# Moving one weight's loads to a second DMA queue in the head of a fused attention and MLP kernel

## The chip, the cores and the metric

The kernel runs on one core of a Trainium2 chip. A core has TensorE (PE in the profile; its weight loads are listed apart as PEld), VectorE (DVE), ScalarE (ACT), GpSimd (POOL) and SyncE (SP). SyncE and ScalarE can both start transfers; here, before the change, SyncE starts all of them. The metric is the device time of one execution in microseconds; smaller is better.

## The reference

Inputs are bfloat16: x of 2048 rows and 512 columns, four 512x512 weights, three weights of a gated MLP with inner width 1792, a vector beta of 32 and a vector gate_w of 512.

```python
x = A_x
g = sigmoid((x * gate_w).sum(-1, keepdims=True))
q, k, v = x @ wq, x @ wk, x @ wv          # 32 heads of 16, 4 segments of 512 rows
for s in range(4):                        # within a segment: causal softmax attention
    a_dot = softmax(q_s k_s^T / 4 + mask) v_s
    a_mem = phi(q_s) M / (phi(q_s) z + 1e-6)      # memory of the segments before
    o_s = sigmoid(beta) * a_mem + (1 - sigmoid(beta)) * a_dot
    M, z = M + phi(k_s)^T v_s, z + sum(phi(k_s))
a = concat(o) @ wo
b = (gelu(x @ w_gate) * (x @ w_up)) @ w_down
out = g * a + (1 - g) * b
```

## The kernel before

Everything works on segments of 512 rows, with x held transposed in the tiles `x0` to `x2`: 128 partitions, 4 chunks `fc` of the 512 columns, 512 rows. Each product with x (`u_k`, `u_q`, `u_v`, `u_gate`, `u_up`) is a group of four matmuls over `fc` into one PSUM bank, and then a copy out of it. A planner in Python, with its own estimates of costs and due times, writes down the order of the instructions of each engine once the head is over; in the head the order is that of the calls. Each engine runs its list in order, and semaphores tie the lists together.

The head is this. `load_inputs` (L136) starts the transfers, all on SyncE: segment 0 of x in two halves of 256 rows, into a borrowed tile `G`; the columns 0 to 255 and 256 to 511 of wk; wq; gate_w; wv; beta; and w_gate in two parts. `cols` (L133) is the helper for weights: a weight's rows are spread over the partitions, so that one contiguous piece is a run of columns of one row: 512 bytes for a half of wk, 1024 bytes for wq, wv and the first part of w_gate, while x comes in pieces of 2048 bytes, beta in pieces of 64 bytes. `warm_up` (L163) gives TensorE matmuls on constants. `transpose_x0` (L177) turns x's two halves with eight TensorE transposes each (tile `x0T`), and per half one VectorE copy (L189) and one ScalarE copy (L191) bring them to SBUF. ScalarE's first instruction is the table load that its first copy needs. Then come three groups with wk (`kT`, L376; groups 0 and 1 read half 0 of wk, group 2 reads half 1), four groups with wq (`qT`, L290), the transposition of gate_w (L195), four groups with wv (`vT`, L414), a narrow group (`zT`, L430), `setup_beta` (L215), which begins with an exponential on ScalarE (L217), and 14 groups with w_gate (`gT`, L473). The later loads, x of segments 1 and 2, w_up, w_down and wo, are started by `load_rest` behind a small VectorE memset (L152).

Eight semaphores are used in turn by the transfers, so the ninth transfer in the program's order waits until the first has landed, the tenth for the second, and so on: the first part of w_gate waits for x's first half, x of segment 1 for the third transfer.

Of the kernel before, what the change touches and what calls it, by code (L numbers as in the profile page):

```python
# [13 lines left out]
P = 128  # L14
D = 512
H = 32
# [16 lines left out]
F32 = dt.float32  # L33
# [20 lines left out]
def kernel(  # L54
# [15 lines left out]
    nc = tc.nc  # L70
# [4 lines left out]
    x2 = A_x[0]  # L75
# [8 lines left out]
    def const(shape, dtype, name):  # L84
        return cpool.tile(shape, dtype, name=name, tag=name)
# [3 lines left out]
    wk = const([P, FC, D], BF, "wk")  # L89
# [8 lines left out]
    beta = const([P, H], BF, "beta")  # L98
# [22 lines left out]
    hm = const([P, 8], F32, "hm")  # L121
# [11 lines left out]
    def cols(dst, src):  # L133
        nc.sync.dma_start(dst[:, :, :], src.rearrange("(fc p) n -> p fc n", p=P))

    def load_inputs():  # L136
        half = L // 2
        for i in range(2):
            nc.sync.dma_start(x0[:, 2 * i:2 * i + 2, :],
                              x2[half * i:half * (i + 1), :].rearrange("(p k) d -> p k d", p=P))  # L140
        for i in range(2):
            n = slice(D // 2 * i, D // 2 * (i + 1))
            cols(wk[:, :, n], A_wk[:, n])
        cols(wq, A_wq)
        nc.sync.dma_start(gw4, gate_w.rearrange("(fc p) -> fc p", p=P))
        cols(wv[:, :, 0:D], A_wv)
        nc.sync.dma_start(beta[:, :], A_beta.rearrange("(o n) -> o n", o=1).to_broadcast((P, H)))
        for n in (slice(0, 4 * P), slice(4 * P, DFF)):
            cols(wga[:, :, n], B_w_gate[:, n])

# [10 lines left out]
    gw4 = G[1][0:FC, KT, 0:P]  # L161
# [535 lines left out]

    ctx.enter_context(tc.manual_schedule())
    load_inputs()
    make_identity(nc, ident[:, :])  # L700
    warm_up()
# [289 lines left out]
    for pieces in visits:  # L991
# [17 lines left out]
        if lumps and lumps[0][0] == clock[0]:  # L1009
            i = lumps.pop(0)[1]  # L1010
# [5 lines left out]
        n = len(visits) - clock[0]  # L1016
# [150 lines left out]
    for reg in flag:  # L1167
        i = 0 if reg.engine == mybir.EngineType.Pool else 1
# [32 lines left out]
```

## Time and profile before

| What | us |
|---|---|
| Median of 3 runs | 269.65 (269.63 to 270.01) |
| Profiled execution, its own time | 270.29 |
| Its span in the profile | 268.6 |
| TensorE busy | 263.5 |
| First transpose of x, first kT matmul, first qT matmul start at | 3.77, 6.05, 9.11 |

The span is the time from the first to the last recorded instruction; the execution's own time holds some more around it. Times in the views are counted from the span's start. A busy TensorE is not TensorE at its peak, since matmuls are pipelined. A row of the timeline gives start, duration, engine, line, operation, output and input, and in brackets the idle time before it and what ended that. SPq rows are the instructions on SyncE that start a transfer; ACTq would be the same on ScalarE.

### The profile page before, as it was taken

The page shows a single profiled execution, that of the slowest core. Times are in us where ns is not written, and L with a number is a line of the kernel's source. Part 1 is how long each engine was busy: PE and PEld are TensorE (multiplying, and loading weights), DVE is VectorE, ACT ScalarE, POOL GpSimd, SP SyncE. Part 2 cuts the span into 40 slices and gives each one's busy share as a digit, 9 for nine tenths or more (in the row PEclk, how much of TensorE's full clock was granted, in tenths as well). Part 3 has the DMA queues.
Part 4 walks back from the last instruction along what each step waited for, and adds up shares of the span by engine and source line. Part 5 has one row for each costly group of instructions (what it writes and reads, how often), then busy time and mean ns, then how long its engine had stood idle before and what let it go on. Part 6 is the DMA issues. An engine that isn't in the chain of part 4 may idle for free.

```text
span 268.6 us, 6586 instructions
## 1 busy us (share of the span) xinstructions
PE 263.5 (98%) x2717; PEld 118.8 (44%) x2717; DVE 203.9 (76%) x392; ACT 209.1 (78%) x163; POOL 156.8 (58%) x298
## 2 busy tenths in 40 slices
PE   7999999999999999999999999999999999999994
PEld 4454444444454444544444444444454544444442
DVE  2899575958778787697985979686889479698374
ACT  4226889999997998889999988889888987657510
POOL 4000158897914979986920998596785069655500
PEclk9999999999999999999999999999999999999999
DMA  7999901200070000300042001100000300002102
GB/s 217 322 202 326 340 13 39 42 4 0 9 156 2 0 21 23 78 4 20 2 61 76 10 21 42 42 20 22 20 23 21 67 2 20 2 20 42 40 22 83
DMA packets 30409, 16.59 MB, mean 62 GB/s; under 512 B 20008, under 2 KB 29096, under 8 KB 30376
## 3 DMA queue, kind: packets, MB, share of 16 engines
q1 hardware_dynamic: 30376, 16.14, 23.1%
q8 instruction: 22, 0.36, 0.6%
q14 instruction: 11, 0.09, 0.1%
HBM read 8.14 MB, written 2.10 MB: 38 GB/s over the span
## 4 chain that ended last, share of the span: by engine, by line
PE 88%; POOL 5%; issue 4%; DVE 1%; ACT 1%; ACTq 0%; DVEq 0%; POOLq 0%
PE gT L473 19%; PE uT L494 17%; PE dT L510 14%; PE lg L649 8%; PE od L674 6%; PE qT L290 5%; PE kT L376 5%; PE aT L532 5%; PE vT L414 4%; POOL pT L658 3%; POOL KTm L386 2%; PE MT L559 1%; PE warm L166 1%; PE mn L628 1%; ACT pT L654 1%
## 5 line engine op out<-in xcount | busy, mean ns | idle before, releaser
L658 POOL TENSOR_SCALAR_AFFINE_SELECT pT<-pT 64x256 bf16<-64x256 bf16 x256 | 113.9, 445 | 94.8 <-ACT pT L654 81.9
L654 ACT ACTIVATE pT<-lg 128x2048 bf16<-128x2048 f32 x72 | 135.1, 1876 | 24.9 <-PE lg L649 21.6
L494 PE MATMUL uT<-x,wup 128*128 128x512 bf16 x224 | 60.4, 380 | 0.0
L473 PE MATMUL gT<-x,wga 128*128 128x512 bf16 x224 | 57.0, 380 | 0.0
L510 PE MATMUL dT<-wdn,G 128*128 128x512 bf16 x224 | 52.9, 380 | 0.0
L500 DVE TENSOR_TENSOR G<-uT,G 128x512 bf16<-128x512 f32 x56 | 38.1, 683 | 6.4 <-PE uT L494 6.2
L386 POOL TENSOR_SCALAR KTm<-ktb,eo 128x512 bf16<-128x512 bf16 x26 | 40.6, 1572 | 1.3
L681 DVE STREAM_TRANSPOSE oq<-od 128x512 f32<-128x512 f32 x32 | 21.0, 695 | 19.3 <-PE od L674 19.3
L510 PEld LDWEIGHTS <-G 128*128 128x128 bf16 x224 | 20.8, 98 | 25.0 <-issue 2.1
L473 PEld LDWEIGHTS <-wga 128*128 128x128 bf16 x224 | 20.4, 98 | 23.9 <-issue 2.2
L494 PEld LDWEIGHTS <-wup 128*128 128x128 bf16 x224 | 19.8, 97 | 24.0 <-issue 5.4
L649 PE MATMUL lg<-QT,KTm 32*128 32x192 bf16 (+7 forms) x512 | 28.6, 287 | 0.0
L313 DVE CAST G<-gT 128x512 bf16<-128x512 f32 x24 | 16.5, 687 | 9.8 <-PE gT L473 9.6
L649 PEld LDWEIGHTS <-KTm 32*128 32x128 bf16 x512 | 8.3, 92 | 28.4 <-issue 28.0
L674 PE MATMUL od<-pT,V 64*32 64x128 bf16 (+7 forms) x512 | 19.4, 284 | 0.2 <-POOL pT L658 0.2
L674 PE MATMUL od<-pT,Vs 64*32 64x128 bf16 (+7 forms) x512 | 19.4, 284 | 0.0
L488 ACT ACTIVATE G<-G 128x3584 bf16<-128x3584 bf16 x6 | 18.8, 3182 | 0.0
L687 DVE SCALAR_TENSOR_TENSOR o<-oq,ogs,rden 128x256 bf16<-128x256 f32 x32 | 17.0, 532 | 1.1
L376 PE MATMUL kT<-x,wk 128*128 128x512 bf16 x64 | 17.2, 388 | 0.4 <-DVE x L189 0.4
L290 PE MATMUL qT<-x,wq 128*128 128x512 bf16 x64 | 16.6, 379 | 0.0
L532 PE MATMUL aT<-wo,oT 128*128 128x512 bf16 (+1 forms) x68 | 16.5, 367 | 0.0
L538 DVE SCALAR_TENSOR_TENSOR tB<-aT,gct,tB 128x512 bf16<-128x512 f32 (+1 forms) x17 | 12.0, 714 | 6.0 <-PE aT L532 5.7
(96 smaller groups left out, 277.2 us busy)
## 6 DMA issues: line engine op xcount, KB each, us to landing
wup<-in_B_w_up_dram SPq DMA_DIRECT2D x1, 1792.0 KB, 8.3
wdn<-in_B_w_down_dram SPq DMA_DIRECT2D x1, 1792.0 KB
out_dram<-tB SPq DMA_DIRECT2D x13, 128.0 KB, 1.7
wga<-in_B_w_gate_dram SPq DMA_DIRECT2D x1, 1280.0 KB, 10.6
Vs<-V SPq DMA_DIRECT2D x8, 144.0 KB, 2.6
G<-in_A_x_dram SPq DMA_DIRECT2D x2, 256.0 KB, 3.0
wk<-in_A_wk_dram SPq DMA_DIRECT2D x2, 256.0 KB, 4.3
wq<-in_A_wq_dram SPq DMA_DIRECT2D x1, 512.0 KB, 5.9
```

The lines of the kernel that those rows point to most:

```text
L290: nc.tensor.matmul(T[:, :], lhsT=wq[:, fc, c * P:(c + 1) * P], rhs=xS[s % NX][:, fc, :], start=(fc == 0), stop=(fc == FC - 1))
L376: nc.tensor.matmul(T[:, :], lhsT=wk[:, fc, c * P:(c + 1) * P], rhs=xS[s % NX][:, fc, :], start=(fc == 0), stop=(fc == FC - 1))
L386: eng.tensor_scalar(out=KTm[:, (NC8 * s + c) % NK, :, p, :], in0=ktb[:, c, :].rearrange("q (b k) -> q b k", b=NB), scalar1=eo[:, p:p + 1], ...
L473: nc.tensor.matmul(T[:, :], lhsT=wga[:, fc, hs * P:(hs + 1) * P], rhs=xS[s % NX][:, fc, :], start=(fc == 0), stop=(fc == FC - 1))
L494: nc.tensor.matmul(T[:, :], lhsT=wup[:, fc, hs * P:(hs + 1) * P], rhs=xS[s % NX][:, fc, :], start=(fc == 0), stop=(fc == FC - 1))
L500: nc.vector.tensor_tensor(out=g, in0=T[:, :], in1=g, op=ALU.mult)
L510: nc.tensor.matmul(T[:, :], lhsT=G[s % NG][:, hs, qt * P:(qt + 1) * P], rhs=wdn[:, hs, :], start=(hs == 0), stop=(hs == HS - 1))
L532: nc.tensor.matmul(T[:, 0:w], lhsT=oT[:, fc, qt * P:(qt + 1) * P], rhs=wo[:, fc, d0:d0 + w], start=(fc == 0), stop=(fc == FC - 1))
L649: nc.tensor.matmul(lg[:, j, off:off + n], lhsT=KTm[rows, i % NK, b].rearrange("r p k -> r (p k)"), rhs=QT[rows, i % NC8, 64 * b:L], start= ...
L654: nc.scalar.activation(pT[:, :, :], lg[:, :, :], AF.Exp, scale=DH ** -0.5)
L658: nc.gpsimd.affine_select(out=v, in_=v, pattern=[[0, 4], [1, 64]], compare_op=ALU.is_ge, fill=0.0, base=0, channel_multiplier=-1)
L674: nc.tensor.matmul(od[p][32 * j:32 * j + 32, 64 * b:L], lhsT=w[:, 18 * h:18 * h + 32], rhs=t[rows, j, off:off + n], start=(b == 0), stop=( ...
```

## The change

In `load_inputs`, the two halves of wk are started by ScalarE, in ScalarE's own DMA queue, behind a copy of a zero into one column of the tile `hm`. SyncE starts x, gate_w and beta, then wq, wv and the two parts of w_gate. The other spelling of x's rearrangement describes the same pieces. All other instructions of all engines stay, in the same order.

```diff
         for i in range(2):
             nc.sync.dma_start(x0[:, 2 * i:2 * i + 2, :],
-                              x2[half * i:half * (i + 1), :].rearrange("(p k) d -> p k d", p=P))
+                              x2[half * i:half * (i + 1), :].rearrange("(p k) d -> p k d", k=2))
+        nc.scalar.copy(hm[:, 0:1], nc.const_aps.tensor(0.0, [P, 1], F32))
         for i in range(2):
             n = slice(D // 2 * i, D // 2 * (i + 1))
-            cols(wk[:, :, n], A_wk[:, n])
+            nc.scalar.dma_start(wk[:, :, n], A_wk[:, n].rearrange("(fc p) n -> p fc n", p=P))
+        nc.sync.dma_start(gw4, gate_w.rearrange("(fc p) -> fc p", p=P))
+        nc.sync.dma_start(beta[:, :], A_beta.rearrange("(o n) -> o n", o=1).to_broadcast((P, H)))
         cols(wq, A_wq)
-        nc.sync.dma_start(gw4, gate_w.rearrange("(fc p) -> fc p", p=P))
         cols(wv[:, :, 0:D], A_wv)
-        nc.sync.dma_start(beta[:, :], A_beta.rearrange("(o n) -> o n", o=1).to_broadcast((P, H)))
         for n in (slice(0, 4 * P), slice(4 * P, DFF)):
             cols(wga[:, :, n], B_w_gate[:, n])
```

## The prediction, on record before the run

> **What bounds the kernel now.** I read the page's first and third parts, then the chain of work that ended last, then the timeline of the first 17 us, then the transfers. Two lines of the page:
>
> ```profile
> PE 263.5 (98%) x2717; PEld 118.8 (44%) x2717; DVE 203.9 (76%) x392; ACT 209.1 (78%) x163; POOL 156.8 (58%) x298
> ...
> q1 hardware_dynamic: 30376, 16.14, 23.1%
> ```
>
> TensorE (PE) is busy 98% of the span. Once it has the first matmuls it hardly stops, so a microsecond that it loses in the head comes out at the end almost whole, and what the other engines or the queues gain there is worth nothing unless PE starts earlier. The second line shows one hardware queue for all transfers of the program: this trace has no stretch in which two queues share the DMA engines. The chain from its start to 13 us (start, length, what):
>
> ```profile
> 0.97 2.31 PE warm L166 x5
> 3.28 0.56 PE warm L172 x15
> 3.84 1.41 PE x0T L183 x12
> 5.25 0.02 issue
> 5.27 0.74 DVE x L189
> 6.01 0.04 issue
> 6.05 3.22 PE kT L376 x12
> 9.27 3.45 PE qT L290 x16
> ```
>
> Warm-up, 16 transposes of x (x0T), VectorE's second copy of x, 12 matmuls with wk (kT), 16 with wq (qT). There is no DMA in it. The timeline shows who issues which transfer and when, and what ScalarE (ACT) does:
>
> ```profile
> 0.79 0.87 SPq L139 DMA_DIRECT2D G<-in_A_x_dram  x2
> 0.85 1.28 ACT L191 ACT_TABLE_LOAD   x1 [0.85 <-PEq L1185]
> ...
> 1.71 0.97 SPq L134 DMA_DIRECT2D wk<-in_A_wk_dram  x2
> ...
> 2.73 0.51 SPq L134 DMA_DIRECT2D wq<-in_A_wq_dram  x1
> ...
> 4.84 1.58 ACT L191 COPY x<-x0T 128x512 bf16<-128x512 bf16 x2 [2.71 <-PE x0T L183]
> ...
> 10.90 0.23 ACT L217 ACTIVATE eb<-beta 128x32 f32<-128x32 bf16 x1 [4.48 <-DMA beta<-in_A_beta_dram]
> ```
>
> The view of one tile gives the times from issue to landing. For wk and for wq:
>
> ```profile
> DMA to landing us min/median/max: 3.5/4.3/5.1
> DMA to landing us min/median/max: 5.9/5.9/5.9
> ```
>
> The reader is to put a deadline beside each landing. x's halves are issued at 0.79 and 1.2 and take 2.8 and 3.1 us: landed at 3.6 and 4.3. The first transpose starts at 3.77, on the heels of the warm-up; the second half is wanted eight transposes later, at 4.60. Slack 0.2 and 0.3 us. wk half 0 is issued at 1.71, landed at 5.2, wanted for the matmul at 6.05: slack 0.85. Half 1 (columns 256 on, the third kT group) is issued at 2.2, landed at 7.3, wanted at 8.25: slack 0.95. wq lands at 8.63 and is wanted at 9.11: slack 0.5. So PE has just enough data at every step, and nothing in the head waits that could be removed.
>
> **The change, part by part.** What it removes: SyncE's queue (SP) no longer issues wk, 0.97 us. What it moves ahead of wq there are gate_w (0.45) and beta (0.50), together 0.95, so wq is issued where it was, at about 2.7. wv comes at about 3.3 instead of 3.78 and wga follows half a microsecond earlier. All of these have slack (wv is wanted at 12.76, wga at 16.28), so on PE's path this saves 0. x's own transfers are issued at the same instants, so x0T cannot start earlier; even with x there at once, the warm-up ends at 3.84. Gain of this part: 0 to 0.07 us; I take 0.
>
> Beta earlier: ACT's 4.48 us of idle time before L217 shrinks. What follows is a table load that then waits 4.91 us for PE, and VectorE uses the result at 17.01. Worth 0. If beta were late again, the cover is these 4.91 us.
>
> What it adds on ACT: a 128x1 copy, priced by the smallest ACT rows (L447, 128x4, 0.20 us; L217 0.23), and two DMA issues, priced by SP's (0.43 and 0.51), 1.2 us in all. Behind them stand the x copies of L191, which now start at 4.84 after 2.71 us of idle time: 1.2 fits, cost 0. The copy needs the table load, which is already the first thing ACT does, so the load moves nowhere. The later SP transfers that reuse wk's semaphore (x of segment 1 at 13.87) wait for a memset of VectorE at 13.77; wk has landed by then in every case below.
>
> What is left is when wk's transfers begin, and with whom they share the DMA engines. That is the whole price, and two numbers in it are not in this trace.
>
> First, the issue time. The new DMA instructions wait for no semaphore. The earliest is 0.85, when ACT starts; the latest is after the table load and the copy, 2.13 + 0.23 = 2.36. SP issued them at 1.71. Data begins about 1.0 us after an issue (x: issued 0.79, the first bytes in the slice of 1.8 to 2.0 us), so wk moves from 1.85 or from 3.36. I take the early end: nothing in the program ties the transfer to the copy's end.
>
> Second, the sharing. In the rows of half a microsecond the DMA engines move 45, 115, 340, 397, 316, 342, 278, 320 GB/s from 1.5 to 5.5 us, and on average 309 from 4 to 8 us: full, and in one order, x (524 KB), wk (524), wq (524). Added up, x is through at 3.74 and lands at 4.33, 0.6 later; wk half 0 is through at 4.53 and lands 0.7 later; half 1 at 5.41, and lands 1.9 later. With two queues wk no longer stands between x and wq but beside them. The ends: it loses nothing to the others and takes nothing from x, cost 0; or it takes half of the bytes from the first moment.
>
> - Early issue, half of the bytes: x's second half is through only when 1049 KB have moved, at 5.41, and lands at 6.0 instead of being ready for 4.60: PE 1.4 us later. wk itself then is in time.
> - Early issue, a fifth of the bytes beside x (x in 2 KB rows, wk in 512-byte rows, one row each in turn): x through after 655 KB, at 4.14, landed at 4.75, 0.15 late. Then wk stands beside wq's 1 KB rows and gets a third, 103 GB/s: half 0 at 5.4, landed 6.1, hidden; half 1 (262 KB, 2.5 us) at 7.95, landed 0.7 to 1.9 later, 8.65 to 9.85 instead of 8.25. PE 0.4 to 1.6 us later.
> - Late issue, half of the bytes: x 0.15 late, half 1 landed by 7.4 to 8.6: PE 0.15 to 0.35 later.
> - Late issue, a row each in turn: half 0 landed at 6.8, half 1 at 9.3 to 10.5: PE 0.75 to 2.25 later.
>
> For the early issue both shares end between 0.4 and 1.6, one through x and one through wk half 1. The 1.4 is too dear by half a microsecond, if PE's slow stretch (rival c) ends at 7.1 whenever kT starts: the 1.0 us from 6.05 holds only 0.5 us of work at full pace. So I take 0.9. wq gets past wk half 1 and is in time; wv and wga, issued earlier, add to what stands beside wk. Beta's 64-byte rows now run right behind x: in the stretch before it landed the rows fall to 176 to 223 GB/s (8.5 to 10 us), some 0.6 us of transfer lost, if beta is what did it. That would delay wq from 8.63 to 9.2, covered when kT is 0.9 late and costing 0.1 where it isn't.
>
> The sum for the profiled execution: span 268.6 + 0.9 = 269.5; its own time was 270.29, 1.69 more than its span, so 271.2. The median of the three runs, 269.65, is 0.64 below the profiled one: 269.65 + 0.9 = 270.55 us.
>
> [...]
>
> **The rivals.** (a) All of it is hidden, the other side: wk, issued early, gets through in the pauses of the first 2.5 us (45 and 115 GB/s, against 340 later), and both halves land before 6.05 and 8.25 without pushing x past 4.60. For it: slack of 0.85 and 0.95 us, which SP's issue time of 1.71 alone cannot fill. Against: from 2.5 us on the engines are full, and wk and wv, wga now compete. It decides at half 1 landing by 8.25. Price 0 to 0.3, time 269.65 to 269.95.
> (b) The copy does hold the issue back to 2.36, and wk, 0.65 us later than before and beside wq, is late for the first kT group: kT starts when half 0 lands, 6.8, and half 1 stops PE again. For it: wk half 1 already took 1.9 us from its last byte to its landing. Against: no wait in the program. Middle of 0.75 to 2.25: +1.5, 271.15.
> (c) Faster. PE's weight loads for kT start at 6.05, 6.43, 6.86, 7.17 and then every 0.22 us: the first three matmuls run slow. If all went at full pace, 0.47 us would be won, with the 0.07 of the transposes 0.54: just 0.2%. Nothing in the change works towards it, and a pause of PE more likely lengthens the slow stretch; 12 matmuls at 0.43 instead of 0.22 would cost 2.5.
>
> **How the numbers follow.** What a measurement of this kernel can tell from no change is about 0.2%, 0.54 us. Early issue with x or wk late, 0.4 to 1.6: chance 0.44, of which a tenth of the whole lies under 0.54. (b), 0.75 to 2.25: 0.21, all slower. (a): 0.25, all within 0.2%. (c) and what I can't name: 0.10. Slower 0.34 + 0.21 + 0.01 of the last, 0.56; within 0.10 + 0.25, 0.35; faster 0.09. The range: the low end, 269.4, leaves out most of (c); the high end, 271.9, is (b) at its 2.25, and leaves out the case that the slow stretch of PE grows too. The likeliest case's own range is 270.05 to 271.25.
>
> **What would show it.** The profile of after has a second hardware queue. The DMA issue on ACT begins before 1.3 (early) or after 2.1 (late). Right: x0T's second half or the third kT group starts late, with a wait for a DMA in front, and qT starts 0.9 later than 9.11. (a) is right if kT and qT start at 6.05 and 9.11. (b): PE's wait stands before the first kT matmul. I am wrong if wk lands earlier than at 5.2 and 7.3 while x keeps its 3.6 and 4.3, or if the difference arises behind 16 us, where I expect the same work in the same order.

## The result and the profile after

The changed kernel takes 271.55 us (median of 10 executions, 270.65 to 274.28), the kernel before 269.92 (10 executions, 269.63 to 270.46). The ratio is 1.0065, with an interval of 1.0044 to 1.0086: slower by 1.6 us. (The ratios take in all executions, so they differ from those of the medians where the executions form groups.) The forecast was 270.55, in a range of 269.4 to 271.9, with slower as the likeliest sign.

The profiled execution of the changed kernel is one of its faster ones: 270.83 us, span 269.1, against 270.29 and 268.6 before. The execution profiled before lies 0.37 over its own median. So the two profiles differ by only 0.5 us of the 1.6, and what the other executions add has to come from the experiments. Lines behind the change stand one lower than in the kernel before. Its page, parts 3 and 4:

```profile
q1 hardware_dynamic: 29320, 15.61, 22.6%
q10 hardware_dynamic: 1056, 0.52, 0.7%
...
PE 85%; POOL 5%; issue 4%; DMA 3%; ACT 1%; SPq 1%; DVE 0%; ACTq 0%; DVEq 0%; POOLq 0%
```

There is a second queue, q10, with wk's 0.52 MB, and a DMA in the chain of work that ended last, where there was none. The chain itself, from its start:

```profile
2.13 0.36 SPq L146
2.48 0.04 issue
2.53 7.00 DMA wq<-in_A_wq_dram
9.53 0.05 issue
9.57 3.63 PE qT L291 x16
```

PE's 16 wq matmuls wait for wq, issued at 2.53 and landed 7.00 us later. Before, wq was issued at 2.73 and took 5.9. The timeline of the head (start, duration, and in brackets the idle time before it):

```profile
0.92 1.00 ACTq L144 DMA_DIRECT2D wk<-in_A_wk_dram  x2
...
2.15 0.19 ACT L141 COPY hm<-const-float32-0.0 128x1 f32<-128x1 f32 x1
...
3.78 1.03 PE L184 MATMUL x0T<-ident,G 128*128 128x128 bf16 x8
...
5.26 0.88 PE L184 MATMUL x0T<-ident,G 128*128 128x128 bf16 x8 [0.45 <-DMA G<-in_A_x_dram]
...
6.68 2.75 PE L377 MATMUL kT<-x,wk 128*128 128x512 bf16 x12 [0.55 <-DVE x L190]
```

The same rows before:

```profile
3.77 1.89 PE L183 MATMUL x0T<-ident,G 128*128 128x128 bf16 x16
...
6.05 3.22 PE L376 MATMUL kT<-x,wk 128*128 128x512 bf16 x12 [0.39 <-DVE x L189]
...
9.11 3.62 PE L290 MATMUL qT<-x,wq 128*128 128x512 bf16 x16
```

wk's transfers are issued at 0.92, long before the copy that stands ahead of them runs at 2.15. The 16 transposes are torn in two: the second eight start at 5.26 instead of 4.60, behind a DMA wait on x. kT starts at 6.68 instead of 6.05. The landings, in the views of the tiles x is loaded into and wk:

```profile
DMA to landing us min/median/max: 2.9/3.5/4.0
DMA to landing us min/median/max: 3.5/4.0/4.5
```

x half 1, issued at 1.25, takes 4.0 us instead of 3.1. wk's halves, issued at 0.92 and about 1.4, land at 4.4 and 5.9: the first before x half 1 (5.25), both earlier than in the kernel before (5.2 and 7.3). Last, busy times and transfer rates by half a microsecond (the last number is GB/s):

```profile
4.50:5.00 0.50, 0.31 (x3) 0.04 (x1) 0.50 (x1) 0.15 (x1) 0.00 (x0) 1.00 1.08 326
5.00:5.50 0.50, 0.24 (x3) 0.25 (x4) 0.15 (x1) 0.50 (x1) 0.00 (x0) 1.00 1.74 138
5.50:6.00 0.50, 0.50 (x8) 0.50 (x6) 0.10 (x1) 0.08 (x1) 0.00 (x0) 1.00 0.59 77
6.00:6.50 0.50, 0.14 (x3) 0.02 (x1) 0.50 (x1) 0.33 (x1) 0.00 (x0) 1.00 0.24 81
6.50:7.00 0.50, 0.32 (x2) 0.19 (x2) 0.23 (x3) 0.40 (x1) 0.00 (x0) 1.00 0.60 209
```

Before, the three rows from 5 to 6.5 us were:

```profile
5.00:5.50 0.50, 0.50 (x7) 0.50 (x5) 0.38 (x2) 0.50 (x1) 0.00 (x0) 1.00 1.15 320
5.50:6.00 0.50, 0.16 (x2) 0.00 (x1) 0.50 (x3) 0.38 (x2) 0.00 (x0) 1.00 0.87 273
6.00:6.50 0.50, 0.45 (x2) 0.17 (x2) 0.10 (x2) 0.42 (x1) 0.00 (x0) 1.00 1.16 344
```

From 5 to 6.5 us, right when wq should be coming in, the engines move 77 to 138 GB/s instead of 273 to 344. The transfer that lies there is beta, landed 5.1 us after its issue at 2.13, at 7.2.

So there are two suspects: wk overtaking x half 1, and beta in front of wq. A third question comes from the spread: six executions of the changed kernel lie at 270.65 to 271.6, and four at 272.1 to 274.3. The slowest, 274.28, had a mean granted clock of 0.991, the other nine 0.998 to 1.0.

### The profile page after: what moved, and what is told of

Its sections match the earlier page's. It is cut to its first block, busy times and chain, and to the rows that moved or that the text cites. A ratio compares the mean times of both kernels' runs of the same rounds, so it can differ in the third digit from the quotient of the medians.

```text
span 269.1 us, 6587 instructions
## 1 busy us (share of the span) xinstructions
PE 263.2 (98%) x2717; PEld 118.4 (44%) x2717; DVE 204.2 (76%) x392; ACT 209.4 (78%) x164; POOL 157.3 (58%) x298
## 4 chain that ended last, share of the span: by engine, by line
PE 85%; POOL 5%; issue 4%; DMA 3%; ACT 1%; SPq 1%; DVE 0%; ACTq 0%; DVEq 0%; POOLq 0%
PE gT L474 19%; PE uT L495 17%; PE dT L511 14%; PE lg L650 8%; PE od L675 6%; PE qT L291 5%; PE aT L533 5%; PE vT L415 4%; PE kT L377 4%; POOL pT L659 3%; DMA wq<-in_A_wq_dram 3%; POOL KTm L387 2%; PE MT L560 1%; PE mn L629 1%; ACT pT L655 1%
## 5 line engine op out<-in xcount | busy, mean ns | idle before, releaser
L480 ACT ACTIVATE G<-gT 128x512 bf16<-128x512 f32 x14 | 8.4, 598 | 12.5 <-PE gT L474 12.5
## 6 DMA issues: line engine op xcount, KB each, us to landing
wga<-in_B_w_gate_dram SPq DMA_DIRECT2D x1, 1280.0 KB, 10.6
```

## The experiments

Each kernel was compared with the kernel before on its own chip; medians of before lay at 269.92 to 269.96. Where a spread is given, it is over all executions.

**e1: beta and gate_w back behind wq.** wk stays in ScalarE's queue.

```diff
-        nc.sync.dma_start(gw4, ...)
-        nc.sync.dma_start(beta[:, :], ...)
         cols(wq, A_wq)
+        nc.sync.dma_start(gw4, ...)
         cols(wv[:, :, 0:D], A_wv)
+        nc.sync.dma_start(beta[:, :], ...)
```

> wk stays in ScalarE's queue, gate_w and beta go back to their old places behind wq and wv. Theory (two causes: wk's early transfers push x half 1 back, and beta's 64-byte pieces in front of wq all but stop the transfers for 1.7 us): x half 1 still lands at about 5.2 and kT starts at about 6.7, but the rows of 5.0 to 6.75 us stay near 300 GB/s, wq lands before 9.2 and TensorE's wait in front of qT is gone; time 0.3 to 0.8 us over before, so about 1 us under the changed kernel. Rival (wk beside x and wq is the whole cause, beta's place is worth nothing): still 1.6 us over before.

Measured: 270.27 us, ratio 1.0037 (1.0018 to 1.0056), 0.32 over before. The profile (270.18 us):

```profile
5.20 0.62 PE L184 MATMUL x0T<-ident,G 128*128 128x128 bf16 x8 [0.39 <-DMA G<-in_A_x_dram]
...
6.41 2.75 PE L377 MATMUL kT<-x,wk 128*128 128x512 bf16 x12 [0.59 <-DVE x L190]
...
9.00 3.62 PE L291 MATMUL qT<-x,wq 128*128 128x512 bf16 x15
```

The torn x0T stays, the wait in front of qT is gone. That is what the theory of two causes expects; the rival, that beta's place is worth nothing, falls. wq is also issued 0.82 us earlier here (1.71 for 2.53); e6 below changes beta alone. But the executions make two groups: seven at 270.18 to 270.27, five at 271.77 to 272.07, and none between.

**e2: beta and gate_w ahead of wq in the kernel before, wk left on SyncE.**

```diff
+        nc.sync.dma_start(gw4, ...)
+        nc.sync.dma_start(beta[:, :], ...)
         cols(wq, A_wq)
-        nc.sync.dma_start(gw4, ...)
         cols(wv[:, :, 0:D], A_wv)
-        nc.sync.dma_start(beta[:, :], ...)
```

> The kernel before with gate_w and beta alone moved ahead of wq; wk stays in SyncE's queue. Theory (two causes): x half 1 lands at 4.3 and kT starts at 6.05 as before; the transfers all but stop for 1.0 to 1.7 us once wk is through, wq lands at 9.5 to 10.3 instead of 8.63, and qT starts 0.4 to 1.2 late; time 0.4 to 1.2 over before. Rival (wk's queue is the whole cause): within 0.2 us of before.

Measured: 271.01 us, ratio 1.0051 (1.0027 to 1.0076), 1.06 over before. Ten executions lie at 270.46 to 271.37, two at 272.62 and 274.49.

```profile
3.77 1.91 PE L183 MATMUL x0T<-ident,G 128*128 128x128 bf16 x16
...
6.07 3.15 PE L376 MATMUL kT<-x,wk 128*128 128x512 bf16 x12 [0.39 <-DVE x L189]
...
9.61 3.63 PE L290 MATMUL qT<-x,wq 128*128 128x512 bf16 x15 [0.39 <-DMA wq<-in_A_wq_dram]
```

x0T is whole and kT starts in time; qT waits for wq and starts 0.50 late. So this place makes the kernel slower without a second queue. But two things move together: wq is also issued 0.91 us later (3.64 for 2.73), and it lands 5.9 us after its issue in both kernels. The transfers do not all but stop, as was expected: they move 149 GB/s from 5.5 to 6 us and 197 to 245 up to 8.5, where the kernel before has 248 to 344. Which of the two costs the time, e2 does not tell.

**e3: e1 with the copy writing into wk, so that wk's transfers wait for it.**

```diff
-        nc.scalar.copy(hm[:, 0:1], nc.const_aps.tensor(0.0, [P, 1], F32))
+        nc.scalar.copy(wk[:, 0, 0:1], nc.const_aps.tensor(0.0, [P, 1], F32))
```

> As e1, but the small copy writes into wk, so that wk's transfers really wait for it. Theory (the plain copy holds nothing back, and an early wk pushes x half 1 back): the issue on ScalarE moves from 0.92 to about 2.4, x half 1 lands at 4.3 to 4.5 again and the second half of x0T has no wait; wk half 0 lands at 5.8 to 6.8, so kT starts between 6.05 and 6.8; time 0 to 0.7 over before, with the wait in front of kT instead of inside x0T. Rival (the wait inside x0T has another cause than wk): x half 1 still lands at 5.2 and the time is that of e1.

Measured: 274.64 us, ratio 1.0167 (1.0147 to 1.0187), 4.7 over before, far more than expected.

```profile
1.71 0.43 SPq L134 DMA_DIRECT2D wq<-in_A_wq_dram  x1
...
2.37 0.98 ACTq L144 DMA_DIRECT2D wk<-in_A_wk_dram  x2
...
3.77 1.89 PE L184 MATMUL x0T<-ident,G 128*128 128x128 bf16 x16
...
8.30 5.28 PE L377 MATMUL kT<-x,wk 128*128 128x512 bf16 x12 [2.64 <-DMA wk<-in_A_wk_dram]
```

The issue moves to 2.37 and x0T is whole again: an early wk was what tore it. But wk, now issued after wq, lands after wq, 5.8 us after its issue (8.2), while wq lands 6.0 after its own (7.7). From 5 to 7 us the two queues ran side by side: ScalarE's moved 0.23 MB, SyncE's 0.44. So wk got a third of the bytes and came 2 us too late for kT. And the 12 kT matmuls take 5.28 us instead of the 2.75 of the changed kernel: all of them run at half pace, after a pause of 2.64.

**e4: the changed kernel without the small copy.**

> The changed kernel without the small copy. Theory (the copy holds nothing back): wk is issued at about 0.85 instead of 0.92, x half 1 lands at about 5.2 again, the table load only moves behind the two issues to about 1.9, under the 2.5 us that ScalarE idles; time within 0.4 us of the changed kernel, 271.2 to 271.9. Rival (the copy or the earlier table load costs or saves something by itself): over 0.5 us from it.

Measured: 270.79 us, ratio 1.0041 (1.0026 to 1.0057); four executions at 270.71 to 270.79, three at 271.6 to 272.1. wk is issued at 0.86 instead of 0.92 and x0T is torn at the same place. The median lies 0.76 under that of the changed kernel, outside of the 0.4 expected, but the lowest executions differ by 0.06 (270.71 and 270.65) and the intervals of the two ratios overlap: the copy holds nothing back, and that it costs something by itself is neither shown nor excluded. The profile is of an execution of 272.05 us:

```profile
6.50 2.75 PE L376 MATMUL kT<-x,wk 128*128 128x512 bf16 x12 [0.59 <-DVE x L189]
...
10.66 3.63 PE L290 MATMUL qT<-x,wq 128*128 128x512 bf16 x15 [1.42 <-DMA wq<-in_A_wq_dram]
```

Here wq comes 8.1 us after its issue at 2.53, and qT starts 1.55 later than in the kernel before, with kT at full pace. The time that beta costs is not a constant: 0.46 late at qT's start in the first profile of the changed kernel, 1.55 in this one.

**e5: e1 with TensorE kept busy in the pause inside x0T.** Two matmuls on constants, into a PSUM bank that nobody reads.

```diff
         for half in range(2):
+            if half == 1:
+                keep_busy((512, 256))
             for f0 in range(0, FC, 2):
```

> As e1 (wk in ScalarE's queue, beta behind wv), with two matmuls on constants (512 and 256 columns, about 0.64 us) between the transposes of x half 0 and those of half 1, where TensorE waits for x half 1. In e1 five of twelve executions took 271.8 to 272.1 and seven 270.2. [...] Rival (the executions at 272 come from late transfers): about as many at 272 as in e1.

Measured: 270.40 us, ratio 1.0018 (1.0009 to 1.0028). All eleven executions lie at 270.27 to 270.76. In e1 it was five of twelve at 272, in e6 below, with the same unfilled pause, six of twelve. The transfers of e5 are those of e1 (x half 1 lands 4.1 us after its issue, 3.9 there), so the counts speak for TensorE's pause and against a late transfer. The profile is of an execution that had reached the full pace before the pause (its first eight transposes take 0.76 us, e1's 1.04): the two matmuls took 0.49 us there, and 0.47 us of waiting was left. No long execution of e1 was profiled, so how the two matmuls keep them away is not shown.

**e6: beta's tile filled from 128 places.**

```diff
-        nc.sync.dma_start(beta[:, :], A_beta.rearrange("(o n) -> o n", o=1).to_broadcast((P, H)))
+        nc.sync.dma_start(beta[:, :], x2[0:P, 0:H])
```

This kernel computes something else, since it gates with numbers of x in beta's place; all instructions and sizes stay.

> The changed kernel, with beta's tile filled from the first 32 columns of x's first 128 rows instead of beta, so that the gate of the memory is another one: the same 128 pieces of 64 bytes, from 128 places in memory instead of one. Theory (what stops the transfers between 5 and 6.75 us is that all 128 pieces read the same 64 bytes): the stop is gone, wq lands before 9.0 instead of 9.53, time 0.4 to 1.2 under the changed kernel. Rival (pieces of 64 bytes are slow as such): the stop stays, 70 to 150 GB/s between 5 and 6.75, and the time is that of the changed kernel.

Measured: 271.21 us, ratio 1.0051 (1.0031 to 1.0072), in two groups like e1's: six executions at 270.18 to 270.47, six at 271.96 to 272.32. The first rows of rates below are those where the changed kernel has 138, 77 and 81 GB/s; the last line is qT's start:

```profile
5.00:5.50 0.50, 0.35 (x7) 0.35 (x8) 0.09 (x1) 0.31 (x1) 0.00 (x0) 1.00 1.08 266
5.50:6.00 0.50, 0.27 (x5) 0.15 (x3) 0.41 (x1) 0.19 (x1) 0.00 (x0) 1.00 1.02 289
6.00:6.50 0.50, 0.13 (x1) 0.10 (x1) 0.41 (x3) 0.50 (x2) 0.00 (x0) 1.00 1.08 362
```

```profile
8.95 3.62 PE L291 MATMUL qT<-x,wq 128*128 128x512 bf16 x16
```

The stop is gone. beta lands 4.0 us after its issue instead of 5.1, wq 5.1 instead of 7.0, and qT does not wait. The pieces have the same size and number, gate_w stays ahead of wq, and wq is issued at 2.52; only beta's source differs. So it is the source that stops the transfers, 128 reads of one place of 64 bytes, and not small pieces, gate_w or wq's issue time. The median missed what was expected because half of the executions fell into the group at 272; the lower group, 270.2, is where the theory put it, and is that of e1.

**e7: the kernel before with its pause between x0T and kT filled.** The same two matmuls, behind x0T.

> The kernel before with two matmuls on constants (512 and 256 columns, about 0.64 us) in TensorE's pause between x0T and kT, 5.40 to 6.05. [...]

Measured: 270.17 us, ratio 0.9999 (0.9978 to 1.0019), eleven executions at 269.83 to 270.48. No gain shows. The median lies 0.21 over before, and the interval allows 0.6 less or 0.5 more, so that the run excludes neither a small gain nor a small cost of the two matmuls.

**e8: e1 with one small transfer ahead of wk in ScalarE's queue,** so that wk is issued after x half 1. It goes to a place that nobody reads.

```diff
         nc.scalar.copy(hm[:, 0:1], nc.const_aps.tensor(0.0, [P, 1], F32))
+        nc.scalar.dma_start(G[1][0:FC, KT + 1, 0:P], gate_w.rearrange("(fc p) -> fc p", p=P))
```

> As e1 (beta behind wv), with one transfer of gate_w into an unused place ahead of wk in ScalarE's queue, so that wk half 0 is issued at about 1.35, after x half 1 (1.25) instead of before it (0.92), and wk half 1 at about 1.8, before wq (about 2.1). Theory (the DMA engines serve the transfers of both queues nearly in the order in which they are issued, in blocks): x half 1 lands at 4.2 to 4.6 and wk halves at about 5.2 and 6 to 7.3; no wait inside x0T; time within 0.25 us of before, and no executions at 272. Rival (the two queues take turns by pieces, so wk always takes a share from x): x half 1 lands at 4.9 to 5.3 again and the time is that of e1.

Measured: 271.21 us, ratio 1.0045 (1.0032 to 1.0058), five executions at 270.70 to 271.25.

```profile
3.77 1.75 PE L185 MATMUL x0T<-ident,G 128*128 128x128 bf16 x16
...
6.05 1.89 PE L378 MATMUL kT<-x,wk 128*128 128x512 bf16 x8 [0.53 <-DVE x L191]
8.61 1.04 PE L378 MATMUL kT<-x,wk 128*128 128x512 bf16 x4 [0.67 <-DMA wk<-in_A_wk_dram]
```

Half of it came as expected: with wk issued at 1.52, after x half 1, x0T is whole, kT starts at 6.05, wk half 0 lands 3.6 us after its issue, and no execution is at 272. But the time is 1.25 over before, outside the 0.25 expected: the third kT group waits for wk half 1, which lands 6.6 us after its issue at about 2.0, at the same time as wq (issued 2.13, 6.7 us). So these two shared the engines. The 0.13 us between their issues do not explain it: in the changed kernel x half 0 and wk half 0 were issued 0.13 us apart as well (0.79 and 0.92), and x half 0 landed 2.9 us after its issue, against 2.8 before. In the profile 0.37 of the loss stands at qT's start (9.48 for 9.11), and the span is 0.8 longer; where the rest arises was not followed up.

**e9: the changed kernel with e5's two matmuls.** beta stays ahead of wq.

> The changed kernel with the two matmuls on constants of e5 in the pause inside x0T; beta stays ahead of wq. [...] Rival (the executions of the changed kernel at 272 and more are due to beta's stop alone): as many of them as before.

Measured: 271.06 us, ratio 1.0048 (1.0024 to 1.0071). Eight executions lie at 270.29 to 271.45, four still at 272.39 to 272.68. That is the rival's count, against four of ten in the changed kernel: filling the pause inside x0T does not take away the long executions while beta stands ahead of wq. e2, which has no pause inside x0T either, has two of twelve. What makes these four long isn't shown by a profile; e4's shows that beta's stop alone can be long enough.

**e10 and e11: the changed kernel and e1 once more, for another profile.**

> The changed kernel itself, for the profile of another execution. [...]

> The kernel of e1 itself, for the profile of another execution. [...] Rival: at 272 a transfer is late and a wait of 1.7 us stands in front of kT or qT.

Both fell into the lower groups, 270.52 and 270.24 us, and look like the first profiles: x0T torn at 5.20 and 5.18, qT at 9.26 and 8.98. They say nothing on the long executions.

**e12: e1 with a longer pause.** gate_w is issued between x's halves, so that x half 1 (1.66) comes after both halves of wk (0.92 and about 1.4).

```diff
+            if i == 1:
+                nc.sync.dma_start(gw4, gate_w.rearrange("(fc p) -> fc p", p=P))
             nc.sync.dma_start(x0[:, 2 * i:2 * i + 2, :], ...)
```

> As e1, with gate_w issued between the two halves of x, so that x half 1 is issued at about 1.7, after both halves of wk (0.92 and 1.40). Theory of the order (transfers are served nearly in the order of their issue): x half 1 lands at 5.8 to 7.3 instead of 4.7 to 5.2, and the pause inside x0T grows from 0.6 to 1.2 to 2.4 us. [...]

Measured: 272.62 us, ratio 1.0089 (1.0056 to 1.0123). One execution at 271.08, five at 272.39 to 273.75. The profile is of one at 272.66:

```profile
5.82 1.03 PE L185 MATMUL x0T<-ident,G 128*128 128x128 bf16 x8 [1.01 <-DMA G<-in_A_x_dram]
...
7.25 4.32 PE L378 MATMUL kT<-x,wk 128*128 128x512 bf16 x12 [0.39 <-DVE x L191]
```

x half 1 lands at 5.8, behind wk half 0 (4.4) and just ahead of half 1 (6.0). And kT's 12 matmuls take 4.32 us where e1 and the changed kernel show 2.75: TensorE runs at half pace until past 10 us, its weight loads 0.43 us apart up to 10.19. That is 1.57 us on top of the pause, about the distance between the two groups of e1. So in this profile the slow pace behind the pause of 1.01 us costs more than the pause itself. That a longer pause makes more executions long is not shown by five of six against five of twelve.

What ends the slow pace stays open. In the kernel before the rows from 6 to 7 us read a granted clock of 1.00 while kT's weight loads start up to 0.43 us apart, and its mean is 0.998 in e12's profiled execution, so no trace here records a cause. And the full pace began at different times where TensorE had done the same until then: within the first eight transposes in the profiles of e4, e5 and e6 (0.76 to 0.82 us for the eight), between the two eights in e1, e10 and e11 (1.03 to 1.04, then 0.62). Before, the slow pace ended at 7.1 us without a waiting transfer, and of the 91 executions of the kernel before on all chips four took 271.8 to 272.1 while all others stayed under 270.8.

None of these kernels is shown to beat the kernel before.

## Why the prediction was right, and where it was off

The sign and the range were right, the size was not: 0.9 us was forecast against a change of 1.63. That the median lies in the range is in part luck. 0.27 of the 1.0 between forecast and result is the base, 269.65 from 3 executions and 269.92 from 10. The term that was to give 0.9, the sharing, gave about 0.3; the rest came from beta, priced at 0 to 0.1, and from long executions, which the range left out. Of the signs, x0T's second half waits for a DMA as forecast, but qT's delay of 0.46 comes from wq, which I had in time.

- *What bounds the kernel, and that nothing in the head can be won.* Right as far as the runs go. x's first transpose starts at 3.78, as it did at 3.77, no run here won anything, and qT's delay came out at the end: 0.46 of 0.5 us of span in the changed kernel, 1.55 of 1.6 in e4, 2.30 of 2.3 in e12.
- *The issue time.* I took the early end of 0.85 to 2.36, since nothing in the program ties the transfers to the copy; it was 0.92, and 0.86 without the copy (e4). The transfers were issued 1.23 us before the copy ahead of them in ScalarE's list ran (2.15), so the list was not run in order here. Rival (b), that the copy holds them, fell.
- *The sharing.* Here the step was wrong. I bounded the loss of x by a half or a fifth of the bytes taken by wk throughout, and by the second expected wk half 1 late. No run shows that fifth, which I had assumed from one row of each queue in turn: by it wk half 0 would have landed at 6.1, and it landed at 4.4. In fact wk half 0, issued between x's halves, went ahead of x half 1 almost whole: x half 1 came 0.9 us later (5.25 for 4.33) and wk half 1 1.4 us earlier than before. In e3 and e8 two transfers did run side by side; what decides between the two ways is not shown. The delay of kT came out at 0.63, between my 0.15 and 1.4, by another way than either.
- *A delay in the slow stretch costs half.* Right in kind: kT started 0.63 late in the profiled execution, but its twelve matmuls then took 2.75 us and not 3.22, since the full pace was there from the first of them. In e1 x half 1 late goes with 0.32 in the median. No profile shows these 0.3: in e1's, qT starts at 9.00, ahead of the 9.11 before, whose profiled execution ran its first three kT matmuls slow and lies 0.37 over its own median.
- *beta ahead of wq.* The largest term that I mis-sized. I took 0.6 us of transfer, worth 0 to 0.1; it holds the engines at 77 to 138 GB/s for 1.5 us and puts wq at 9.53 instead of 9.2 (at 10.6 in e4's profile); its place alone, gate_w and wq's later issue included, costs 1.06 in e2. I had read a row of 64-byte pieces behind other queued work, where the dip was shallow (176 to 223 GB/s), and carried it to another place in the order.
- *The slow stretch of PE, rival (c).* I named what a pause could cost, 2.5 us, and left it out of the sum and of the range. e1, where beta is back, has 0.32 in its median and 1.7 more in five of twelve executions. The changed kernel spreads over 3.6 us, and four of its ten executions lie over my range, while the median lies inside. Why they are so long is open: with the pause filled four of twelve still are as long (e9), e4's profile at 272.05 has kT at full pace and a late wq, and the slowest, 274.28, had the lower granted clock.

The parts, as far as the runs separate them: x half 1 late, 0.3 us (e1's lower group, 270.2, against 269.95); beta, 0.4 to 1.4 more (270.65 to 271.6, the changed kernel's lower group, against 270.2); and more in the executions over 271.8, four of ten. In e1 and e6 I put the long executions down to the slow pace, by the count of e5 and the profile of e12; none of them was profiled. In the changed kernel itself the slow pace and beta's stop weren't told apart, since e9 kept its four long executions; that stays open.

## What to carry to other kernels

The second DMA queue added no bandwidth here (336 GB/s on average from 2.5 to 5 us, 335 before); it changed the order, and where one queue already delivers every tile a few tenths of a microsecond before its use, a new order can only be late. Look at what the moved transfer overtakes by its issue time, instruction by instruction: here the issue came 1.23 us before the copy in front of it ran, and behind it, at 2.37, only where the copy wrote into the transfer's tile (e3). A small broadcast load goes behind all transfers that somebody waits for soon: beta ahead of wq put qT's start 0.46 to 1.55 us later in the profiles. And a pause of TensorE in the first 10 us is to be priced with the half-pace matmuls that may follow it: 1.57 us behind a pause of 1.01 (e12), 2.53 behind one of 2.64 (e3).

## What was not expected of the hardware

- 128 pieces of 64 bytes that all read one place all but stopped the DMA engines: 77 to 138 GB/s in the rows from 5 to 6.5 us. As many pieces of the same size from 128 places left 266 to 362 GB/s (e6).
- Two hardware queues did not share in one fixed way. A transfer issued 0.33 us earlier on the other queue landed before the later one (wk half 0 at 4.4, x half 1 at 5.25), while in e3 and e8 transfers of the two queues ran side by side (in e8 both landed at 8.6 to 8.8).
- With a pause of 0.4 to 0.6 us between the two eights of transposes, 11 of 24 executions were some 1.7 us longer than the others (e1, e6), with one of 1.0 us five of six (e12), and after one of 2.64 us 12 matmuls took 5.28 us instead of 2.75 (e3). The mean granted clock was 0.998 in e12's profiled execution and 1.0 in e3's, so that no trace here shows what made the matmuls slow.
